# Reordering three groups of loads and casts in a windowed-attention and gated-FFN kernel

## The chip, the core and the metric

The kernel runs on one core of one Trainium2 chip. The metric is the device time of one execution in microseconds (us). It is taken over several runs, and one further execution is profiled.

The engines are named as in the profile: PE is TensorE (matmuls; PEld its weight loads), ACT is ScalarE, DVE is VectorE, POOL is GpSimd, and SP is SyncE, which here only issues DMAs. A "q" behind an engine's name means its instruction queue, which issues DMAs and waits.

## The reference

Attention over a batch of 4, with 8 heads, 768 positions and a head size of 64. Each position sees the first 4 positions (sinks) and the last 128. Its output, laid out as 3072 tokens by 512, goes through a gated feed-forward network:

```python
scores = scale * np.matmul(q, k.transpose(0, 1, 3, 2))
keep = is_sink | in_window              # rel = i - j, 0 <= rel < 128
a = softmax(np.where(keep, scores, -1e9))
x = np.matmul(a, v)                     # -> (3072, 512)
gate = np.maximum(x @ w_gate, 0.0)      # 512 x 1536
return (gate * (x @ w_val)) @ w_out     # 1536 x 512
```

All inputs and the output are float32 in device memory. The products run in bfloat16.

## The kernel before, in words

**Units.** The heads are taken in pairs, so a batch has four units, and there are 16 units U[0] to U[15]. Unit i belongs to batch i // 4 and pair i % 4. Of each unit the kernel needs the queries and keys turned to head size by position (`KQ`), the exponentials of the scores (`ee`), the product with the values (`xn`), and that product turned back (`xT`).

**Batch 0.** Its queries and keys come in eight halves: half c is pair c % 4, with c // 4 telling which half of the positions. `load_half` (L110) issues one load of k and one of q. `cast_half` (L116) casts them on GpSimd to bfloat16. `T_half` (L262) turns them on TensorE. So half 5 is the second half of pair 1. The float32 buffers `kf` and `qf` have three places, and half 5 uses the second part of the third.

**Batches 1 to 3.** Whole units are loaded by `load_rows` (L159) and cast by `cast_rows` (L164, on GpSimd). Batch 1 is turned on TensorE. For batches 2 and 3, `to_dram` (L169) writes the cast rows back to memory and `turn` (L174) reads them transposed. After that GpSimd copies "odd tiles" and sinks inside the keys (`odd_tiles` L183, `sinks` L179, the copies of L185 and L181), and the scores read those copies. `x_to_dram` (L147) and `x_turn` (L154) turn the attention output of batches 2 and 3 in the same way.

**Values.** There are seven value tiles a batch. `load_v` (L124) loads tile j with one DMA for even j and three for odd j, and `cast_v` (L133) casts it into `vn`, on GpSimd unless another engine is given. `W` (L310) is the product of exponentials and values. In batch 0 it is done in two parts: part 0 needs value tiles 0 to 2, part 1 needs tiles 3 to 6. In the other batches it needs all seven.

**Weights.** `load_w(m0, m1)` (L188) asks GpSimd's DMA queue for columns m0 to m1 (in blocks of 128) of `w_gate` and `w_val`, cast to bfloat16 on the way.

**The order.** Everything is in a hand-written order (`manual_schedule`), and each engine takes its instructions in program order. First comes an opening (L412 to L462) that brings up batch 0. Then follow 96 slots (L467): slot s does one `chunk` (L350), which is block m of the first FFN layer for one half of a batch's tokens: four matmuls with `w_gate`, four with `w_val` (L362), a relu on ACT (L377) and a product on DVE (L379). After its chunk, a slot does the attention steps that `plan` gives it ("S" scores, "W" value product, "X" and "T" turns, "H" turn of a half) and some matmuls of the second FFN layer (`ffn2`, L404). Ahead of its chunk, a slot does what `prep` gives it (L495 to L515): loads, casts and copies for later slots, in the order of the slot's list. Slots 0 to 23 are the FFN of batch 0, slots 24 to 47 of batch 1, and so on. Slot s of batch b runs while the attention of batch b + 1 is made.

Around the change the plan reads: slot 1 "S04 H1", slot 2 "S02 H2 S14", slot 6 "W01 W11" for batch 0 (L477); slot 29 "S00 S01", slot 31 "S02 S10", slot 35 "W0 S20" for batch 2 (L488). The scores of batch 0's first parts and the first value products stand in the opening. The row casts of unit 12 are in slot 33 (L504), and the odd tiles of a unit are copied in the slot ahead of its first scores (L508).

**Waits between engines** come from the data: a reader waits for its writer, a writer of a buffer for the buffer's readers. The memset of a corner of a float32 buffer (L138, L449) is used on purpose as a gate: it stands at a chosen point of DVE's order, and the load that overwrites the corner waits for it. Loads on SP share eight completion semaphores in turn, so a load on SP also waits until the load eight places earlier has landed.

Of the kernel before, what the change touches and what calls it, by code (L numbers as in the profile page):

```python
# [21 lines left out]
def kernel(  # L22
# [12 lines left out]
    nc = tc.nc  # L35
# [16 lines left out]
    kf = [const.tile([128, S], F32, name=f"kf{i}") for i in range(NQ)]  # L52
# [55 lines left out]
    half = lambda bufs, c: bufs[c // 2 % len(bufs)][:, c % 2 * HALF:c % 2 * HALF + HALF]  # L108

    def load_half(c, queues=(nc.sync, nc.sync)):  # L110
        p, x = c % NP, c // NP
        for src, bufs, queue in ((k, kf, queues[0]), (q, qf, queues[1])):
            queue.dma_start(out=half(bufs, c).rearrange("p (h e) -> p h e", h=2),
                              in_=src[0, 2 * p:2 * p + 2, x * HALF:x * HALF + HALF].rearrange("h (p n) d -> p h (n d)", n=3))

    def cast_half(c, copies=(nc.gpsimd.tensor_copy, nc.gpsimd.tensor_copy)):  # L116
        for src, dst, copy in ((kf, kn, copies[0]), (qf, qn, copies[1])):
            copy(half(dst, c).rearrange("p (n h d) -> p h n d", n=3, h=2),
                                  half(src, c).rearrange("p (h n d) -> p h n d", n=3, h=2))
# [4 lines left out]
    def load_v(b, j, r0=0, r1=128):  # L124
        r1 = min(r1, S - VROW[j])

        parts = [(0, 4, 0), (4, 16, VROW[j] + 4), (16, 128, VROW[j] + 16)] if j in (1, 3, 5) else [(0, 128, VROW[j])]
        for a0, a1, s0 in parts:
            a1 = min(a1, r1)
            if r0 <= a0 < a1:  # L130
                nc.sync.dma_start(out=vf[a0:a1, j, :, :], in_=v[b, :, s0:s0 + a1 - a0, :].rearrange("h s d -> s h d"))  # L131

    def cast_v(b, j, rows=128, copy=nc.gpsimd.tensor_copy):  # L133
        copy(vn[b % 2][0:rows, j, :, 0:64], vf[0:rows, j, :, :])  # L134
# [53 lines left out]
    def load_w(m0, m1, which=(0, 1)):  # L188
        for w, dst in (((moe_w_gate, wg), (moe_w_val, wv))[x] for x in which):
            nc.gpsimd.dma_start(out=dst[:, :, m0 * 128:m1 * 128],  # L190
                                in_=w.rearrange("(ko ki) n -> ki ko n", ki=128)[:, :, m0 * 128:m1 * 128])
# [5 lines left out]
    def setup():  # L197
        nc.vector.memset(warm[:], 0.0)
        nc.scalar.activation(warm[:], warm[:], Act.Exp, bias=0.0, scale=1.0)
        make_identity(nc, ident)  # L200

        nc.gpsimd.memset(band[:], 1.0)
        nc.gpsimd.affine_select(out=band[:], in_=band[:], compare_op=Alu.is_ge, fill=0.0, base=0,
                                pattern=[[1, 256]], channel_multiplier=-1)
        nc.gpsimd.affine_select(out=band[:], in_=band[:], compare_op=Alu.is_ge, fill=0.0, base=127,
                                pattern=[[-1, 256]], channel_multiplier=1)
        for c0, c1, x0 in ((8, 252, 0), (504, 507, 244)):
            nc.gpsimd.affine_select(out=msk[:, 0, c0:c1], in_=band[:, x0:x0 + c1 - c0], compare_op=Alu.is_ge, fill=0.0,
                                    base=119, pattern=[[0, c1 - c0]], channel_multiplier=-1)
        nc.gpsimd.memset(vf[:, 6, :, :], 0.0)  # L210
        cp, ms = nc.vector.tensor_copy, nc.vector.memset
        for i in range(NE):
            ms(ee[i][:, 0, :, 507:640], 0.0)
            ms(ee[i][:, 0, :, 0:8], 1.0)
        ms(vn[0][:, :, :, 64:66], 1.0)
        cp(msk[:, 0, 252:504], band[:, 4:256])
        ms(msk[0:4, 0, 252:504], 1.0)
        ms(msk[0:4, 0, 8:128], 1.0)
        ms(msk[0:4, 0, 128:252], 0.0)
        ms(msk[0:4, 0, 504:507], 0.0)  # L220
        bias(mb[:, 0, 8:507], msk[:, 0, 8:507])
        bias(mb[:, 1, 0:128], band[:, 0:128])
# [56 lines left out]
    def Sg(u, s, ps=None):  # L279
        t, bias = u.i % NT, u.b == 0 and s in (0, 3)  # L280
        g, b0, n, segs = SEG[s]
        ps = ps or pair()
        at = [ps[h][:] if isinstance(ps, list) else ps[:, h, :] for h in range(2)]
        if bias:
            for h in range(2):
                nc.tensor.matmul(out=at[h][:, b0:n], lhsT=ident[:], rhs=mb[:, g, b0:n], start=True, stop=False,
                                 skip_group_check=True)
        for x0, q0, c0, c1 in segs:
            for h in range(2):
                nc.tensor.matmul(out=at[h][:, c0:c1], lhsT=kE[t][64 * h:64 * h + 64, x0:x0 + 128],  # L290
                                 rhs=qT[t][64 * h:64 * h + 64, q0:q0 + c1 - c0], start=not bias, stop=True,
                                 skip_group_check=True)
        x = ee[u.i % NE][:, g, :, b0:n]
        if isinstance(ps, list):
            for h in range(2):
                nc.scalar.activation(x[:, h, :], at[h][:, b0:n], Act.Exp, bias=0.0, scale=scale)
        else:
            nc.scalar.activation(x, ps[:, :, b0:n], Act.Exp, bias=0.0, scale=scale)  # L298
        if not bias:
            nc.vector.tensor_tensor(x, x, msk[:, g, b0:n].unsqueeze(1).to_broadcast([128, 2, n - b0]), op=Alu.mult)  # L300
# [110 lines left out]
    with tc.manual_schedule():  # L411
# [3 lines left out]
            load_half(c, (nc.sync, nc.scalar))  # L415
        for j in range(3):
            load_v(0, j)
        for c in (4, 5):
            load_half(c)
        setup()  # L420
        g = [x[:] for x in G]
        dve = nc.vector.tensor_copy
# [13 lines left out]
        load_w(0, 2)  # L436
        for j in range(3):
            cast_v(0, j, copy=dve if j == 2 else nc.gpsimd.tensor_copy)
        load_w(2, 4)
        cast_half(4)  # L440
        cast_half(5)
        load_w(4, 6)
        Sg(U[2], 0, PP[1])
        Sg(U[2], 3, PP[0])
        W(U[0], 0, g[2])
# [47 lines left out]
                for y in w.split():  # L493
                    put(s, y, b)
        prep = [[] for _ in slots]  # L495
        prep[1] += [("half", 6), ("w", 6, 8), ("half", 7), ("setup3",), ("v", 0, 3), ("v", 0, 4), ("v", 0, 5), ("v", 0, 6)]
        prep[4] += [("load", 4), ("load", 5), ("load", 6)]
        prep[8] += [("kq", 4), ("load", 7), ("lv", 1), ("kq", 5), ("w", 8, 12)]
        prep[10] += [("kq", 6)]
# [9 lines left out]
            prep[at["W", i, 0] + 1].append(("xd", i))  # L509
            prep[at["W", i, 0] + 3].append(("xturn", i))  # L510

        for b, s0, s1 in ((2, 23, 28), (3, 44, 47)):
            for j in range(7):
                prep[s0 + j].append(("lv", b, j))
                prep[s1 + j].append(("v", b, j))  # L515

        f2 = deque()
        mid = {0: lambda: X(U[3], 0, g0), 8: lambda: X(U[3], 1)}
# [96 lines left out]
```

## Time and profile before

| | |
|---|---|
| median of 5 runs | 253.09 us (251.38 to 254.8) |
| the profiled execution, its own time | 254.61 us |
| its span in the profile | 252.6 us |
| granted TensorE clock, mean | 0.992 |
| TensorE busy | 239.1 us, 95% |
| DVE, ACT, GpSimd busy | 115.6, 120.6, 68.6 us |
| DMA | 40.07 MB, mean 159 GB/s |
| DMA queues: SP's, GpSimd's | 34.10 MB, 4.72 MB |
| chain that ended last: PE, DMA | 80%, 12% |

The span is the time from the first to the last instruction of the program; the execution's own time has about 2 us around it. Times "at" a moment are us from the start of the span. In lists of waits, the figures are total us, number of times, and the longest. In timelines, a bracket at the end of a line gives the idle time of the engine just before, and what ended it. The releaser is inferred from semaphore events. The DMA share of a stretch is the mean busy share of the core's 16 DMA engines; it can pass 1 since transfers overlap.

### The profile page before, as it was taken

The page shows a single profiled execution, that of the slowest core. Times are in us where ns is not written, and L with a number is a line of the kernel's source. Part 1 is how long each engine was busy: PE and PEld are TensorE (multiplying, and loading weights), DVE is VectorE, ACT ScalarE, POOL GpSimd, SP SyncE. Part 2 cuts the span into 40 slices and gives each one's busy share as a digit, 9 for nine tenths or more (in the row PEclk, how much of TensorE's full clock was granted, in tenths as well). Part 3 has the DMA queues.
Part 4 walks back from the last instruction along what each step waited for, and adds up shares of the span by engine and source line. Part 5 has one row for each costly group of instructions (what it writes and reads, how often), then busy time and mean ns, then how long its engine had stood idle before and what let it go on. Part 6 is the DMA issues. An engine that isn't in the chain of part 4 may idle for free.

```text
span 252.6 us, 5300 instructions
## 1 busy us (share of the span) xinstructions
PE 239.1 (95%) x2063; PEld 140.5 (56%) x2084; DVE 115.6 (46%) x224; ACT 120.6 (48%) x220; POOL 68.6 (27%) x125
## 2 busy tenths in 40 slices
PE   7879979999999997999999999999999999999994
PEld 3455566656765554566555556665555555555443
DVE  5465863788752443466434555734232223222000
ACT  3849927997343564453335754531333323333111
POOL 7775663982534305521003610000000000000000
PEclk9999999999999999799999999999999999999999
DMA  6999999999999999598899602334211011110232
GB/s 201 246 212 248 244 344 245 209 186 234 328 255 231 250 213 382 177 190 200 205 179 244 132 18 57 101 76 114 74 44 42 0 42 45 43 42 0 86 125 83
DMA packets 75681, 40.07 MB, mean 159 GB/s; under 512 B 53512, under 2 KB 72712, under 8 KB 75656
## 3 DMA queue, kind: packets, MB, share of 16 engines
q1 hardware_dynamic: 67560, 34.10, 52.3%
q0 software_dynamic: 6864, 4.72, 12.6%
q10 hardware_dynamic: 1232, 0.92, 1.1%
q8 instruction: 16, 0.26, 0.4%
q14 instruction: 9, 0.07, 0.1%
HBM read 28.48 MB, written 11.25 MB: 157 GB/s over the span
## 4 chain that ended last, share of the span: by engine, by line
PE 80%; DMA 12%; SPq 2%; issue 2%; POOL 1%; DVE 1%; ACT 1%; ACTq 0%; POOLq 0%; DVEq 0%
PE g L362 44%; PE g L404 19%; PE pp L325 5%; DMA vf<-in_v_dram 5%; DMA qf<-in_q_dram 4%; PE pp L290 4%; PE pp L404 3%; DMA kf<-in_k_dram 2%; SPq L131 1%; POOL vn L134 1%; PE g L342 1%; SPq L161 1%; PE pp L254 1%; PE g L254 1%; PE pp L398 1%
## 5 line engine op out<-in xcount | busy, mean ns | idle before, releaser
L379 DVE TENSOR_TENSOR hT<-gs,g 128x384 bf16<-128x384 f32 (+2 forms) x96 | 53.0, 552 | 89.7 <-PE g L362 81.2
L377 ACT ACTIVATE gs<-g 128x384 f32<-128x384 f32 (+2 forms) x96 | 47.7, 497 | 77.6 <-PE g L362 76.5
L362 PE MATMUL g<-xT,wv 128*128 128x384 bf16 (+2 forms) x384 | 79.1, 327 | 2.2 <-DMA wv<-in_moe_w_val_dram 2.2
L362 PE MATMUL g<-xT,wg 128*128 128x384 bf16 (+2 forms) x384 | 79.5, 328 | 0.5 <-ACT xT L345 0.5
L404 PE MATMUL g<-wo,hT 128*128 128x512 bf16 x219 | 61.0, 382 | 1.7 <-issue 0.5
L362 PEld LDWEIGHTS <-wg 128*128 128x128 bf16 x384 | 36.3, 98 | 31.1 <-issue 0.9
L362 PEld LDWEIGHTS <-wv 128*128 128x128 bf16 x384 | 37.5, 98 | 28.9 <-DMA wv<-in_moe_w_val_dram 3.1
L298 ACT ACTIVATE ee<-pp 128x838 bf16<-128x838 f32 (+4 forms) x50 | 43.0, 904 | 10.4 <-PE pp L290 9.9
L404 PEld LDWEIGHTS <-hT 128*128 128x128 bf16 x276 | 25.6, 98 | 24.1 <-issue 1.1
L300 DVE TENSOR_TENSOR ee<-ee,msk 128x838 bf16<-128x838 bf16 (+3 forms) x44 | 31.2, 711 | 14.2 <-ACT ee L298 13.4
L134 POOL CAST vn<-vf 128x512 bf16<-128x512 f32 x27 | 18.0, 682 | 32.7 <-DMA vf<-in_v_dram 32.7
L325 PEld LDWEIGHTS <-ee 128*128 128x128 bf16 x512 | 18.1, 97 | 5.5 <-issue 3.7
L325 PE MATMUL pp<-vn,ee 128*128 128x65 bf16 x488 | 18.1, 193 | 2.4 <-POOL vn L134 2.4
L408 ACT COPY ot<-g 128x512 f32<-128x512 f32 x20 | 11.7, 587 | 17.5 <-PE g L404 17.5
L331 DVE TENSOR_TENSOR xn<-pp,rn 128x896 bf16<-128x896 f32 (+2 forms) x18 | 17.0, 943 | 0.6
L290 PEld LDWEIGHTS <-KQ 64*128 64x128 bf16 x328 | 10.9, 94 | 10.2 <-issue 7.9
L290 PE MATMUL pp<-KQ 64*128 64x3 bf16 (+5 forms) x316 | 16.0, 222 | 0.0
L166 POOL CAST kn<-kf 128x768 bf16<-128x768 f32 x12 | 9.9, 828 | 19.2 <-DMA kf<-in_k_dram 10.8
L166 POOL CAST qn<-qf 128x768 bf16<-128x768 f32 x12 | 10.4, 865 | 3.5 <-DMA qf<-in_q_dram 3.4
L185 POOL COPY KQ<-KQ 128x372 bf16<-128x372 bf16 x12 | 6.8, 567 | 14.1 <-PE g L362 6.4
L345 ACT COPY xT<-g 128x372 bf16<-128x372 bf16 (+2 forms) x10 | 5.4, 545 | 7.2 <-PE g L342 7.2
L404 PE MATMUL pp<-wo,hT 128*128 128x512 bf16 x36 | 8.1, 379 | 0.0
(80 smaller groups left out, 107.0 us busy)
## 6 DMA issues: line engine op xcount, KB each, us to landing
out_dram<-ot SPq DMA_DIRECT2D x23, 256.0 KB
kf<-in_k_dram SPq DMA_DIRECT2D x12, 384.0 KB
qf<-in_q_dram SPq DMA_DIRECT2D x12, 384.0 KB
vf<-in_v_dram SPq DMA_DIRECT2D x12, 256.0 KB
vf<-in_v_dram SPq DMA_DIRECT2D x12, 224.0 KB
kf<-in_k_dram SPq DMA_DIRECT2D x8, 192.0 KB
wo<-in_moe_w_out_dram POOLq DMA_DIRECT2D x3, 512.0 KB, 9.1
kqd<-qn SPq DMA_DIRECT2D x8, 192.0 KB
```

The costliest lines, as they stand in the source:

```text
L134: copy(vn[b % 2][0:rows, j, :, 0:64], vf[0:rows, j, :, :])
L166: nc.gpsimd.tensor_copy(dst[u.i % 2][:].rearrange("p (n h d) -> p h n d", n=NR, h=2), src[u.i % NQ][:].rearrange("p (h n d) -> p h n d", n ...
L290: nc.tensor.matmul(out=at[h][:, c0:c1], lhsT=kE[t][64 * h:64 * h + 64, x0:x0 + 128], rhs=qT[t][64 * h:64 * h + 64, q0:q0 + c1 - c0], start ...
L298: nc.scalar.activation(x, ps[:, :, b0:n], Act.Exp, bias=0.0, scale=scale)
L300: nc.vector.tensor_tensor(x, x, msk[:, g, b0:n].unsqueeze(1).to_broadcast([128, 2, n - b0]), op=Alu.mult)
L325: nc.tensor.matmul(out=at[h][:, c:c + 65], lhsT=ee[u.i % NE][:, g, h, c0:c0 + 128], rhs=vn[u.b % 2][:, j, 2 * u.p + h, 0:65], start=c == 0 ...
L331: nc.vector.tensor_tensor(x.rearrange("p t (h d) -> p h t d", h=2), o[:, :, :, 0:64], r.unsqueeze(3).to_broadcast([128, 2, n, 64]), op=Alu ...
L362: nc.tensor.matmul(out=ps[:, 0:n], lhsT=w[:, ko, m * 128:(m + 1) * 128], rhs=x[:, ko, c], start=ko == 0, stop=ko == KO - 1)
L377: nc.scalar.activation(gs[:, 0:n], gp[:, 0:n], Act.Relu, bias=0.0, scale=1.0)
L379: nc.vector.tensor_tensor(h[:, m, c], gs[:, 0:n], vp[:, 0:n], op=Alu.mult)
L404: nc.tensor.matmul(out=op, lhsT=hT[b % 2][:, m, t * 128:(t + 1) * 128], rhs=wo[:, m, :], start=m == 0, stop=m == FM - 1)
L408: nc.scalar.copy(ot[:], op)
```

## The change

There are three edits.

1. The load of half 5 is taken out of the opening's first loads. It now stands behind the casts of value tiles 0 to 2, with a memset of its corner on DVE ahead of it, so that SP issues it once DVE has passed its own cast of value tile 2.
2. The loads of weights 4 and 5 are asked for ahead of the cast of half 5, and those of weights 6 and 7 ahead of the cast of half 6.
3. The casts of batch 2's value tiles 0 to 6 move from slots 28 to 34 into slots 27 to 33, and each stands first in its slot's list instead of last. Their loads stay where they were. The casts of batch 3 stay as they were.

```diff
         for j in range(3):
             load_v(0, j)
-        for c in (4, 5):
-            load_half(c)
+        load_half(4)
         setup()
...
         for j in range(3):
             cast_v(0, j, copy=dve if j == 2 else nc.gpsimd.tensor_copy)
+
+        nc.vector.memset(half(kf, 5)[0:1, 0:2], 0.0)
+        load_half(5)
         load_w(2, 4)
         cast_half(4)
+        load_w(4, 6)
         cast_half(5)
-        load_w(4, 6)
         Sg(U[2], 0, PP[1])
...
-        prep[1] += [("half", 6), ("w", 6, 8), ("half", 7), ("setup3",), ("v", 0, 3), ("v", 0, 4), ("v", 0, 5), ("v", 0, 6)]
+        prep[1] += [("w", 6, 8), ("half", 6), ("half", 7), ("setup3",), ("v", 0, 3), ("v", 0, 4), ("v", 0, 5), ("v", 0, 6)]
...
-        for b, s0, s1 in ((2, 23, 28), (3, 44, 47)):
+        for b, s0, s1 in ((2, 23, 27), (3, 44, 47)):
             for j in range(7):
                 prep[s0 + j].append(("lv", b, j))
-                prep[s1 + j].append(("v", b, j))
+                prep[s1 + j].insert(0 if b == 2 else len(prep[s1 + j]), ("v", b, j))
```

## The prediction

> **What bounds the kernel now.** I read the page first (TensorE busy 239.1 of 252.6 us), then the chain of waits by line, then who waits for whom on TensorE, then the timeline at the places that the diff touches. The waits on TensorE:
>
> ```profile
> PE pp L325 <- POOL vn L134: 2.4, 4, 1.0
> PE g L362 <- DMA wv<-in_moe_w_val_dram: 2.2, 2, 1.1
> ```
>
> So TensorE sets the end, and it loses time at few places: at the value casts (total us, times, longest us) and at two weight loads. The opening, from the timeline of TensorE (start, us, work, idle before it and its releaser):
>
> ```profile
> 18.22 0.49 PE L362 MATMUL g<-xT,wv 128*128 128x372 bf16 x2 [1.05 <-DMA wv<-in_moe_w_val_dram]
> 32.41 0.80 PE L362 MATMUL g<-xT,wv 128*128 128x372 bf16 x4 [1.12 <-DMA wv<-in_moe_w_val_dram]
> 33.61 0.22 PE L325 MATMUL pp<-vn,ee 128*128 128x65 bf16 x2 [0.21 <-POOL vn L134]
> 34.17 1.12 PE L325 MATMUL pp<-vn,ee 128*128 128x65 bf16 x32 [0.34 <-POOL vn L134]
> ```
>
> Two weight waits, then a release by the value casts at 34.17. The second place is slot 35, the first value product of batch 2. The timeline of GpSimd there:
>
> ```profile
> 88.32 0.61 POOL L134 CAST vn<-vf 128x512 bf16<-128x512 f32 x1 [0.90 <-DMA vf<-in_v_dram]
> 97.39 0.83 POOL L166 CAST kn<-kf 128x768 bf16<-128x768 f32 x1 [8.45 <-DMA kf<-in_k_dram]
> 98.42 0.83 POOL L166 CAST qn<-qf 128x768 bf16<-128x768 f32 x1 [0.21 <-DMA qf<-in_q_dram]
> 99.19 0.61 POOL L134 CAST vn<-vf 128x512 bf16<-128x512 f32 x1
> 99.75 0.50 POOL L185 COPY KQ<-KQ 128x372 bf16<-128x372 bf16 x1
> 100.19 0.19 POOL L181 COPY KQ<-KQ 128x12 bf16<-128x12 bf16 x1
> 100.33 0.61 POOL L134 CAST vn<-vf 128x512 bf16<-128x512 f32 x1
> ```
>
> GpSimd stands 8.45 us at the key cast of unit 12, and the last two value casts (tiles 5 and 6) stand behind it. They were asked for at 87.71 to 89.47, and the completion events in the trace put their landing at 92.2 and 92.3. What TensorE does meanwhile, from the same timeline:
>
> ```profile
> 99.86 0.22 PE L325 MATMUL pp<-vn,ee 128*128 128x65 bf16 x2 [0.97 <-POOL vn L134]
> 100.99 0.70 PE L325 MATMUL pp<-vn,ee 128*128 128x65 bf16 x18 [0.91 <-POOL vn L134]
> ```
>
> And its clock by the microsecond (the granted clock is the first figure after the busy times):
>
> ```profile
> 101.00:102.00 1.00, 1.00 (x24) 0.80 (x23) 0.25 (x1) 0.00 (x0) 1.00 (x2) 0.88 0.88 328
> 102.00:103.00 1.00, 0.78 (x6) 0.39 (x4) 0.99 (x1) 0.82 (x1) 1.00 (x3) 0.50 0.20 71
> 103.00:104.00 1.00, 1.00 (x4) 0.37 (x4) 0.79 (x2) 0.18 (x1) 0.06 (x1) 0.50 0.07 25
> 104.00:105.00 1.00, 1.00 (x5) 0.48 (x4) 0.00 (x0) 0.16 (x1) 0.34 (x1) 0.50 0.61 146
> 105.00:106.00 1.00, 1.00 (x14) 0.51 (x14) 0.20 (x1) 0.33 (x1) 1.00 (x2) 0.91 0.62 133
> ```
>
> Nearly 2 us of standing are followed by half a clock from about 101.8 to 105.2. The missing clock adds up to 0.12 + 0.5 + 0.5 + 0.5 + 0.09 = 1.71 us.
>
> **What the Trainium skill says.** "TensorE: Matmul & The Clock Gate", What's actually happening: the clock falls to half after a mostly idle window of 3413 ns and returns after a busy one; the windows run freely. The trace agrees in the half (0.50) and the length (3.4 us), and shows that about 2 us of idleness can do it. Same page, Architectural detail: GpSimd takes its queue strictly in order; the 8.45 us agree. "DMA: Bandwidth & Descriptors", Issuing engines are not separate DMA queues: loads from SP and GpSimd share the same 16 engines; and Queues, rings and completion order: an engine takes turns among its queues. The trace agrees: from 12 us to 34 us the DMA share is at or above 1.0.
>
> **The change, part by part.**
>
> *Batch 2's values a slot sooner, ahead of their slot's other work.* Same seven casts of 0.61 us. Tile 6 now stands in slot 33 ahead of unit 12's row casts, tile 5 in slot 32. Both run at 92.2 to 93.4 in what was GpSimd's idle 8.45 us. Slot 35's product then runs at 98.35 in 0.97 us, as the other 32-matmul products do, instead of until 101.69: 3.34 - 0.97 = 2.37 us saved. Late next: scores S20 of the same slot read unit 10's odd tiles, which GpSimd copies after unit 12's casts. Those end at about 99.2 as before, since their load sets them; the copies follow without the value cast between, 99.19 + 0.44 + 0.19 = 99.82. The product ends at 99.32 and S20's first pair takes about 0.15, so its second pair waits 0.35 to 0.4 us. Net 1.97 us. With one short wait the clock should hold. From the product's end to the next chunk's end took 105.70 - 101.69 = 4.0 us; at full clock scores 0.5, three FFN2 matmuls 0.7 and chunk 1.30 make 2.5. That is 1.5 us more; in runs of before whose clock held, this part is nothing.
>
> What the sooner casts push back: unit 8's odd-tile copy now stands behind value tiles 0 and 1 (tile 1 landed at 81.0), so it ends at 82.4 instead of 78.6; its scores start at 84.79. Unit 9's stands behind tiles 2 and 3 (tile 3 landed at 86.5), so it ends at 87.9; its scores start at 89.35. Both cost nothing, with 2.4 and 1.4 us of cover; each us beyond costs a us. SP's order is untouched here. Afterwards SP is nearly continuously issuing from 110.7 to 133, and the last turned x of batch 2 landed at 132.2, 0.2 us before its chunk at 132.40. SP's stretch starts when slot 37's product is normalised, so it moves up with TensorE; I count no loss, at most 1 us.
>
> *Half 5 asked for behind the first values.* One DVE memset (0.06 us, the row of L449) behind the third value cast, which ends at 12.29 + 0.48 = 12.77. The k load goes out at about 12.9 instead of 10.12, q at 13.4 instead of 10.63. Behind it on SP stands only half 6, which waits for its own memset until 15.2 anyway. Memset cost: nothing, DVE idles until 13.34. The first weights get the engines alone meanwhile. k and q of half 5 are 0.39 MB at some 0.32 MB/us, 1.2 us. So wv for slots 0 and 1 lands about 1.1 us sooner and the 1.05 us wait at 18.22 goes. Half 5 was cast by 17.7 and is transposed at 21.8; 2 to 2.5 us later it still fits.
>
> *Weights ahead of casts.* Each pair of loads holds GpSimd 1.5 us (0.74 + 0.75). Weights 4 and 5 go out near 14.9 instead of 17.64, 6 and 7 near 19.5 instead of 22.96. The casts behind each pair start 1.5 us later and land within the waits for their loads.
>
> *What of that reaches the end.* Product W01 at 34.17 waits for value tiles 3 to 6 of batch 0, which land at about 33 because the same bytes (weights 0 to 7, eight halves, all values) have to pass full engines first. A reordering doesn't shorten this sum. So TensorE arrives 1 to 2 us sooner and waits as much longer: 0 gained, between -1 (values land sooner because weights no longer trail on some engines) and +1.7 (the longer standing halves the clock for one window).
>
> **Sum.** 1.97 + 1.5 + 0 = 3.5 us. Against the profiled execution's own 254.61 (span 252.6 and 2.0 around it) that is 251.1. The median of the five runs, 253.09, is 1.5 lower; they spread over 3.4 us, which fits a clock drop that not every run has, so at the median 2.0 to 3.5 is gained. I take 3.2: 249.9.
>
> **Rivals.**
> *Both places gain.* Values land 1 us sooner and W01 follows. For: weights trail on some engines to 32.4. Against: full engines. 253.09 - 4.3 = 248.8.
> *The opening gives back.* The longer standing before W01 (some 2.5 us, where 1.12 + 0.55 stood) costs half a clock, 1.5 us: 249.9 + 1.5 = 251.4. For: 1.9 us did it at slot 35. Against: windows run freely and need not fall so.
> *The wait moves to S20.* The row load of unit 12, or its copies, come a us or more later relative to TensorE, the wait is as long as before and the clock falls too: under 1 us is left, 252.3. Against: its load is issued by SP, whose chain starts at a gate that TensorE's progress opens, near 60 us.
> *Slower: weights push the values.* With weights 6 and 7 queued 3.5 us sooner the weight queue never runs dry (it nearly did at 19 to 21), and the values of batch 0 give way by a full pair: 0.52 MB at 0.185 MB/us (the rate in 16 to 18, with weights alone) is 2.8 us, plus half a clock after it, 1.5: 249.9 + 4.3 = 254.2. It decides from a landing 3.2 us late, after 36.2. Against: those weights passed ahead of the last values before, too.
> That the change does nothing: excluded for the casts, whose order is GpSimd's program order.
>
> **How the numbers follow.** Forecast 0.55 (its own range 248.8 to 251.0), both gain 0.13, opening gives back 0.17, wait moves 0.09, slower 0.06. Leaving out a tenth on each side gives 248.4 to 252.8. One per cent, about what a measurement of this kernel can tell from no change, is 2.5 us, so faster begins at 250.6: three quarters of the forecast, all of "both", a fifth of "gives back": 0.57. Slower (above 255.6) 0.04, the far ends of the last two rivals; the rest 0.39.
>
> **What would show it.** Right: value casts of tiles 5 and 6 ahead of the 8 us gap on GpSimd; no wait for vn in slot 35; at most 0.5 us before S20; clock 1.00 through 106; wait at 18.22 gone; W01 still released by a value cast near 34. Wrong: a new TensorE wait for unit 8's or 9's odd tiles, a half clock near 34 to 38, or value tile 5 of batch 0 cast much after 33.

## The result, and the profile after

The changed kernel takes 253.29 us (median of 44 runs, 251.14 to 257.13) where the kernel before, run beside it, takes 252.88 (79 runs, 250.93 to 256.38). The ratio is 1.0019, 95% interval 1.0002 to 1.0036: no gain, where 3.2 us were forecast. Here and below, ratios leave out the runs that took over 1.5% longer than the fastest run of their kernel, while the medians are over all runs. The profiled execution of the changed kernel took 252.6 us by its own time, with a span of 250.5 and a granted clock of 1.000.

That is 2 us below the profiled execution of before (254.61), and still no gain: the profile of before was one of the longer executions of its kernel. The table sets them side by side with a second profile of before (before_again) and others that are used below. A slot's start is its first matmul of L362. Each column is one execution.

| start of (us) | before | before_again | after | after_timed | third edit alone (values_again) |
|---|---|---|---|---|---|
| slot 7 | 35.12 | 34.39 | 34.44 | 35.75 | 34.91 |
| slot 19 | 60.77 | 60.03 | 60.07 | 61.39 | 60.55 |
| slot 20 | 63.19 | 63.14 | 63.64 | 66.08 | 62.98 |
| slot 35 | 97.05 | 97.00 | 97.49 | 99.94 | 96.84 |
| slot 36 | 103.31 | 101.73 | 101.04 | 103.29 | 100.19 |
| slot 52 | 141.56 | 139.15 | 139.46 | 140.61 | 137.51 |
| end of the span | 252.57 | 250.18 | 250.46 | 251.61 | 248.51 |

The waits on TensorE of the changed kernel (total us, times, longest):

```profile
PE pp L325 <- POOL vn L134: 1.9, 4, 0.7
...
PE pp L290 <- POOL KQ L181: 0.6, 1, 0.6
...
PE g L362 <- DMA xT<-xd: 0.3, 1, 0.3
```

The weight loads (wv) have left the list. The value casts are still there, with 1.9 us where 2.4 stood, so either the third edit failed or they wait elsewhere. The timeline of GpSimd ahead of slot 35 shows that the edit did what it says:

```profile
93.56 1.18 POOL L134 CAST vn<-vf 128x512 bf16<-128x512 f32 x2 [2.97 <-DMA vf<-in_v_dram]
97.55 0.83 POOL L166 CAST kn<-kf 128x768 bf16<-128x768 f32 x1 [2.81 <-DMA kf<-in_k_dram]
98.70 0.83 POOL L166 CAST qn<-qf 128x768 bf16<-128x768 f32 x1 [0.33 <-DMA qf<-in_q_dram]
99.47 0.50 POOL L185 COPY KQ<-KQ 128x372 bf16<-128x372 bf16 x1
99.91 0.20 POOL L181 COPY KQ<-KQ 128x12 bf16<-128x12 bf16 x1
```

Tiles 5 and 6 are cast by 94.74, ahead of the row casts of unit 12. TensorE there, and its clock by the microsecond:

```profile
98.79 1.13 PE L325 MATMUL pp<-vn,ee 128*128 128x65 bf16 x32
99.86 0.59 PE L290 MATMUL pp<-KQ 64*128 64x244 bf16 x6
```

```profile
101.00:102.00 1.00, 1.00 (x7) 0.59 (x6) 0.79 (x2) 0.62 (x2) 0.82 (x2) 1.00 1.05 395
102.00:103.00 1.00, 1.00 (x19) 0.58 (x17) 0.61 (x2) 0.50 (x2) 1.00 (x2) 1.00 1.10 408
```

The product runs in one piece, S20 waits for 0.2 us at most, the clock stays at 1.00. In the opening the wait at 18.22 is gone (the first line, the same two matmuls, has no bracket) and W01 is released by a value cast again, at 33.47 where it was 34.17:

```profile
16.71 0.48 PE L362 MATMUL g<-xT,wv 128*128 128x372 bf16 x2
...
32.55 0.22 PE L325 MATMUL pp<-vn,ee 128*128 128x65 bf16 x2 [0.39 <-POOL vn L134]
33.47 1.12 PE L325 MATMUL pp<-vn,ee 128*128 128x65 bf16 x32 [0.70 <-POOL vn L134]
```

All this is as forecast. What was not is slot 19, where batch 1's first value product stands. Its line in the kernel before, and its lines in the changed one:

```profile
62.23 1.13 PE L325 MATMUL pp<-vn,ee 128*128 128x65 bf16 x32
```

```profile
62.54 0.22 PE L325 MATMUL pp<-vn,ee 128*128 128x65 bf16 x2 [0.48 <-POOL vn L134]
63.10 0.70 PE L325 MATMUL pp<-vn,ee 128*128 128x65 bf16 x18 [0.34 <-POOL vn L134]
```

Before, nothing waits. After, TensorE waits twice for the last two value tiles of batch 1; from slot 19 to slot 20 it takes 3.57 us instead of 2.42. In the table the same stretch takes 4.69 us in after_timed. The casts of these tiles on GpSimd wait for their loads, in both kernels; the last one before, then the last two after:

```profile
61.97 0.61 POOL L134 CAST vn<-vf 128x512 bf16<-128x512 f32 x1 [0.36 <-DMA vf<-in_v_dram]
```

```profile
61.88 1.17 POOL L134 CAST vn<-vf 128x512 bf16<-128x512 f32 x2 [5.75 <-DMA vf<-in_v_dram]
```

The last cast ends at 62.58 before and at 63.05 after, 0.47 us later. The rest of the new wait is there because TensorE reaches slot 19 0.70 us sooner in this profile. So what counts is how late slot 20 begins.

The later loads begin in SP's timeline (start, us, work, count). Before, then after:

```profile
18.29 9.07 SPq L131 DMA_DIRECT2D vf<-in_v_dram  x8
27.45 0.39 SPq L161 DMA_DIRECT2D kf<-in_k_dram  x1
```

```profile
18.05 11.52 SPq L131 DMA_DIRECT2D vf<-in_v_dram  x8
29.67 0.39 SPq L161 DMA_DIRECT2D kf<-in_k_dram  x1
```

SP issues the last eight DMAs of batch 0's values from nearly the same moment, but it needs 11.52 us for them instead of 9.07, and so the first rows of batch 1 (L161) are asked for 2.2 us later. Nearly all of it is the issues' own time (10.81 and 8.46 us); it is not the wait for the load eight places earlier, since the longest issue, 4.17 us from 21.74, began after the last signal of that load at 21.63.

The delay of the issue does not go on to the end of the queue: the last row load and the first value load of batch 1 go out at 35.87 and 36.28 after, and at 36.04 and 36.46 before. The bytes are behind for longer: by 36 us the queue of SP had moved 5.87 MB before and 5.46 after, by 40 us 7.17 and 6.98, and by 44 us the same (7.64 and 7.63). The issue of the last value load of batch 1 ends at 51.17 before and at 51.75 after. At that time w_out begins to pass, asked for by GpSimd, and the values that are left come slowly: in the profile of before SP's queue moved only some 0.27 MB from 52 to 60 us, where it had moved 0.34 a us at 32 to 40. So a small lateness there has a price.

### The profile page after: what moved, and what is told of

The parts are those of the page before. It is cut to its first block, busy times and chain, and to the rows that moved or that the text cites. A ratio compares the mean times of both kernels' runs of the same rounds, so it can differ in the third digit from the quotient of the medians.

```text
span 250.5 us, 5303 instructions
## 1 busy us (share of the span) xinstructions
PE 237.4 (95%) x2063; PEld 140.1 (56%) x2084; DVE 115.8 (46%) x225; ACT 120.9 (48%) x220; POOL 69.9 (28%) x125
## 3 DMA queue, kind: packets, MB, share of 16 engines
q1 hardware_dynamic: 67560, 34.10, 52.7%
## 4 chain that ended last, share of the span: by engine, by line
PE 70%; DMA 20%; SPq 4%; issue 2%; POOL 1%; DVE 1%; ACTq 0%; ACT 0%; POOLq 0%; DVEq 0%
PE g L362 37%; PE g L404 19%; DMA vf<-in_v_dram 14%; PE pp L325 5%; DMA qf<-in_q_dram 4%; PE pp L404 3%; SPq L131 3%; PE pp L290 3%; DMA xd<-xn 1%; DMA xT<-xd 1%; SPq L113 1%; PE pp L398 1%; PE g L398 1%; POOL vn L134 1%; PE g L342 0%
## 5 line engine op out<-in xcount | busy, mean ns | idle before, releaser
L362 PE MATMUL g<-xT,wg 128*128 128x384 bf16 (+2 forms) x384 | 79.0, 326 | 0.8 <-ACT xT L345 0.5
L362 PE MATMUL g<-xT,wv 128*128 128x384 bf16 (+2 forms) x384 | 78.7, 326 | 0.0
L362 PEld LDWEIGHTS <-wg 128*128 128x128 bf16 x384 | 36.1, 98 | 30.3
L362 PEld LDWEIGHTS <-wv 128*128 128x128 bf16 x384 | 37.6, 98 | 26.2 <-issue 1.8
L134 POOL CAST vn<-vf 128x512 bf16<-128x512 f32 x27 | 18.7, 711 | 40.2 <-DMA vf<-in_v_dram 40.2
```

The costliest lines, as they stand in the source:

```text
L362: nc.tensor.matmul(out=ps[:, 0:n], lhsT=w[:, ko, m * 128:(m + 1) * 128], rhs=x[:, ko, c], start=ko == 0, stop=ko == KO - 1)
```

## The experiments

**Both kernels once more.** No edit; a second profile of each, because the profile of before held a half clock.

> The kernel before, profiled once more on another occasion. If its first profile is typical (theory A: the late value casts and the half clock in slot 35 are in most executions), it shows a wait of 1.5 to 2.5 us for vn in slot 35 and a half-clock window near 102 again, span near 252.6. If its first profile was an unlucky one (theory B), there is no half clock there, slot 48's chunk starts 1.5 to 3 us sooner than 132.2, and a wait for the turned x or for odd tiles shows in slots 48 to 51, which the first profile did not have.

> The changed kernel, profiled once more. Both theories: no wait for vn in slot 35, a wait before S20 of 0.1 to 1 us at most, and waits of 0.3 to 1.5 us in all in slots 48 to 51, where the first profile of it had a wait for the turned x (0.34) and for unit 13's odd tiles (0.64).

Measured: 252.2 us (span 250.2) and 252.46 (span 250.3). The second profile of before has slot 35's wait, but no half clock:

```profile
100.11 0.70 PE L325 MATMUL pp<-vn,ee 128*128 128x65 bf16 x18 [0.91 <-POOL vn L134]
```

That is between the two theories. Slots 35 to 36 take 4.73 us in it, 1.38 above the 3.35 of values_again; in the profile that the prediction was read from they took 6.26. After_again loses 2.1 us at slot 19.

**The edits apart.** The third edit alone, and the first two alone.

```diff
-        for b, s0, s1 in ((2, 23, 28), (3, 44, 47)):
+        for b, s0, s1 in ((2, 23, 27), (3, 44, 47)):
...
-                prep[s1 + j].append(("v", b, j))
+                prep[s1 + j].insert(0 if b == 2 else len(prep[s1 + j]), ("v", b, j))
```

> Edit 3 alone: batch 2's value casts a slot sooner and first in their slots. Theory A (the gain is there, and the opening gives it back): 0.8 to 1.4% faster, ratio 0.986 to 0.992. Theory B (a later wait, set by SP's queue and by the order on GpSimd in slots 48 to 51, takes what slot 35 gains): ratio 0.997 to 1.002, with no vn wait in slot 35 and new TensorE waits at slots 48 to 51.

Measured: 0.9937 of before (0.9905 to 0.9969), 251.45 against 253.47 us, between the two theories.

> Edits 1 and 2 alone: half 5 gated and the weights ahead of the casts. Theory A: 0.8 to 1.4% slower, ratio 1.008 to 1.014, through a half clock near 34 or value tiles 3 to 6 landing later than 33. Theory B: ratio 0.999 to 1.004; the wait at 18 for wv is gone, and the release of W01 stays within 1 us of 34.2.

Measured: 1.0025 (0.9996 to 1.0054), theory B's range, with W01 at 34.36. Its profile loses 0.83 us at slot 19, and at slot 35 only 0.7 are lost instead of 1.38: slot 35 begins later, and waits less. Slot 36 begins at 102.13, against 101.73 in before_again.

So the third edit gains 0.6% by itself, and with the other two beside it the gain is gone, though these two alone cost only 0.25%, with an interval that holds 1. They were then divided. Edit 1 alone (half 5 behind the first values):

```diff
-        for c in (4, 5):
-            load_half(c)
+        load_half(4)
...
+        nc.vector.memset(half(kf, 5)[0:1, 0:2], 0.0)
+        load_half(5)
```

> Edit 1 alone: half 5 asked for behind the first values, the order of weights and casts as before. If the weights' order carries the opening's cost (theory C1), ratio 0.996 to 1.001, with the wv wait near 17 gone and SP's queue at least 6.5 MB in by 36 us. If the late half carries it (theory C2, SP's queue stands empty from 12 to 16 us and never catches up), ratio 1.002 to 1.006 and about 6.2 MB by 36 us.

Edit 2 alone (weights ahead of casts):

```diff
         load_w(2, 4)
         cast_half(4)
+        load_w(4, 6)
         cast_half(5)
-        load_w(4, 6)
...
-        prep[1] += [("half", 6), ("w", 6, 8), ("half", 7), ...
+        prep[1] += [("w", 6, 8), ("half", 6), ("half", 7), ...
```

> Edit 2 alone: weights 4 to 7 ahead of the casts, half 5 asked for as before. Theory C1 (the value loads, packets of 256 B, ride alone behind the weights and pass slower than beside them): ratio 1.002 to 1.006, W01's release 34.2 or later. Theory C2: 0.996 to 1.001.

Measured: 1.0025 (0.9995 to 1.0054) and 1.0026 (1.0003 to 1.0049). The first ratio is what theory C2 said, the second what C1 said, so neither theory holds for both, and a cost of edit 1 isn't shown. The profiles differ. With edit 1 alone the weights stand behind casts that now come later, and TensorE pays in the opening (in an execution of 255.45 us, where the median is 253.48):

```profile
35.30 1.11 PE L362 MATMUL g<-xT,wv 128*128 128x372 bf16 x3 [2.86 <-DMA wv<-in_moe_w_val_dram]
```

SP issues its eight value DMAs in 6.22 us there. With edit 2 alone TensorE waits for no weights behind slot 0 (0.83 us there), but the eight take 11.96 us. So it is the sooner weights that hold SP up. This profile of edit 2 loses only 0.23 us at slot 19, so the hold-up alone does not fix what is lost there.

**Is slot 19 the place? The loads of w_out moved.** GpSimd asks for w_out in three loads ahead of batch 1's value casts; here they stand between casts 4 and 5, in the kernel with the third edit alone and in the changed one.

```diff
-        prep[13] += [("wo",)]
-        prep[14] += [("v", 1, 0), ("v", 1, 1), ("v", 1, 2), ("v", 1, 3), ("v", 1, 4), ("v", 1, 5), ("v", 1, 6)]
+        prep[14] += [("v", 1, 0), ("v", 1, 1), ("v", 1, 2), ("v", 1, 3), ("v", 1, 4), ("wo",), ("v", 1, 5), ("v", 1, 6)]
```

> Edit 3, and the three loads of w_out moved on GpSimd from slot 13 to between the value casts 4 and 5 of batch 1 (slot 14), where GpSimd arrives near 56.8 instead of 49. Theory C (slot 19's wait for batch 1's last values is a floor that the DMA engines set, since w_out passes beside tile 5): tile 5 lands at 57 to 59.5 instead of 61 to 63, no vn wait in slot 19, slot 20 starts by 63.2, ratio 0.988 to 0.993. Theory D (the floor is elsewhere): slot 20 unchanged and the ratio as for edit 3 alone, 0.992 to 0.996, or above if w_out is now late for the second FFN layer.

> The changed kernel with the same move of w_out. Theory C (the opening's cost acts only through slot 19's floor): within 0.3% of the run with edit 3 and the move, ratio 0.987 to 0.994. Theory D (the opening edits cost on their own, by a half clock or by later values of batch 0): 0.5% or more slower than that run.

Measured: 1.0167 (1.011 to 1.0224) and 1.019 (1.0148 to 1.0232). Both are slower than either theory said. The wait at slot 19 is gone in both, so w_out's bytes take part in it. But the lateness has only moved on; TensorE in slot 29 of the first kernel (the second has 3.75 us there):

```profile
87.55 0.85 PE L290 MATMUL pp<-KQ 64*128 64x252 bf16 x10 [3.38 <-POOL KQ L181]
```

Unit 8's odd tiles are late, since their copy on GpSimd stands behind value tiles 0 and 1 of batch 2, and tile 1 lands late: its cast begins at 86.30, the copy at 86.86. That is the wait for unit 8's odd tiles that the prediction named as a sign of being wrong. (The expectations further down speak of slot 31 and unit 9 for it.)

**Repeats, and two variants of the third edit.** The third edit alone and the changed kernel again without an edit; then only tiles 5 and 6 sooner; then the third edit with two places of small waits moved, unit 10's odd tiles ahead of unit 12's row casts and batch 3's value casts a slot later.

```diff
-                prep[s1 + j].append(("v", b, j))
+                if b == 2 and j > 4:
+                    prep[s1 - 1 + j].insert(0, ("v", b, j))
+                else:
+                    prep[s1 + j].append(("v", b, j))
```

```diff
-            prep[at["S", i, 0] - 1].append(("sinks", i))
+            if i == 10:
+                prep[33].insert(0, ("sinks", i))
+            else:
+                prep[at["S", i, 0] - 1].append(("sinks", i))
...
-        for b, s0, s1 in ((2, 23, 27), (3, 44, 47)):
+        for b, s0, s1 in ((2, 23, 27), (3, 44, 48)):
```

> Edit 3 alone, timed a second time beside the changed kernel. Theory E (edit 3 gains where the wait of slot 35 stands and the opening's two edits then take it back): ratio 0.990 to 0.997 again, at least 0.4% below the changed kernel of this job. Theory F (the two belong to different occasions and the first difference was chance): within 0.3% of the changed kernel.

> The changed kernel beside it. Theory E: ratio 0.998 to 1.004, and slot 7 and slot 20 of its profile later than those of edit 3 alone by some 0.5 us. Theory F: ratio as for edit 3 alone.

> Of edit 3 only value tiles 5 and 6 of batch 2, put first in slots 32 and 33; tiles 0 to 4 stay where they were. Theory G (the gain is only that these two stand ahead of unit 12's row casts): the same ratio as edit 3 alone within 0.3%, 0.990 to 0.997, no vn wait in slot 35. Rival (the sooner casts of tiles 0 to 4 matter, or cost): more than 0.4% off.

> Edit 3, with unit 10's odd-tile copy also put ahead of unit 12's row casts (front of slot 33), and the value casts of batch 3 a slot later (slots 48 to 54), behind unit 13's odd tiles. Theory H (what takes slot 35's place is S20's wait for that copy and slot 50's for unit 13's): no wait before S20 and none for odd tiles in slot 50, 0.2 to 0.4% below edit 3 alone, ratio 0.987 to 0.994. Rival (the loads, not the order on GpSimd, end last there): no difference to edit 3 alone beyond 0.2%.

Measured: 0.9969 (0.9939 to 0.9999), 1.002 (0.9995 to 1.0045), 0.9976 (0.9953 to 0.9998) and 0.9964 (0.9941 to 0.9988). So the gain came again, with an interval that ends just short of 1. Tiles 5 and 6 alone are within the interval of the whole edit, and in their profile slot 35 has no wait for a value cast. But it waits 1.06 us before S20 there (102.53), because unit 12's row cast came at 100.09, 2.5 us later than the 97.55 of the changed kernel; this execution had a half clock in the opening. The changed kernel's small waits at slots 48 to 51 (the 0.3 and 0.6 us in its list) are not what takes the gain back: without such places the third edit is no better. Slot 19 of after_timed:

```profile
64.99 0.22 PE L325 MATMUL pp<-vn,ee 128*128 128x65 bf16 x2 [1.60 <-POOL vn L134]
```

From slot 19 to 20 the four profiles with the whole opening and w_out in its place lose 0.83, 1.15, 2.10 and 2.27 us, 1.6 in the mean. The six with neither of its edits lose 0.3 in the mean (four of them nothing, before_again 0.69, values_only 1.17). Two of these four reach slot 19 some 2 us later than the rest, with a half clock behind them, which hides a wait. Without them it is four against four: slot 7 begins at 34.9 in the mean without the opening's edits and at 35.0 with them, slot 20 at 63.4 and at 64.7. That is 1.3 us, most of it at slot 19.

**Does the opening cost anywhere else?** First with the least move, one w_out load behind the last value cast of batch 1, on the third edit alone and on the changed kernel:

```diff
-        prep[13] += [("wo",)]
-        prep[14] += [("v", 1, 0), ... ("v", 1, 6)]
+        prep[13] += [("wo", 0, 1)]
+        prep[14] += [("v", 1, 0), ... ("v", 1, 6), ("wo", 2)]
```

> The third edit alone (batch 2's values sooner), and only the third load of w_out is moved, from slot 13 to behind value cast 6 of batch 1 in slot 14. Theory (what the opening's edits cost, they cost through slot 19, where TensorE waits for batch 1's last values): here that wait is at most 0.1 us, and the time is 0.990 to 0.997 of the kernel before, with no new wait at slot 31. Rival (a debt of the transfers that only changes its place): TensorE waits 1 us or more at slot 31 for unit 9's odd tiles, as it did when all three loads were moved, and the time is 1.000 to 1.010.

> The changed kernel with all three edits, and the same move of the third load of w_out. Theory (slot 19 is the only way by which the opening's edits reach the end): the wait at slot 19 falls from 1.2 to 2.3 us to at most 0.5, and this kernel comes within 0.3% of the run beside it that has the third edit alone with the same move. Rival (they cost elsewhere, in the clock or later): slot 19 has no wait, and this kernel is still 0.5% or more slower than the run beside it. Second rival: the debt only changes its place, and slot 31 waits 1 us or more in both.

Measured: 1.0064 (1.0025 to 1.0102) and 1.0058 (1.0031 to 1.0086). The two agree, but this doesn't decide: TensorE waits for odd tiles at later slots in both (1.8 us at slots 35 and 50 in the first, 3.0 at slots 29, 31 and 35 in the second). The debt has moved on, though not to slot 31 in both as the second rival said, and a wait that takes in a delay can hide a difference. So bytes were taken out instead. First one of the three loads:

```diff
-                                         rhs=wo[:, i, c], start=i == 0, stop=i == FM - 1)
+                                         rhs=wo[:, i % 8, c], start=i == 0, stop=i == FM - 1)
...
-        nc.tensor.matmul(out=op, lhsT=hT[b % 2][:, m, t * 128:(t + 1) * 128], rhs=wo[:, m, :],
+        nc.tensor.matmul(out=op, lhsT=hT[b % 2][:, m, t * 128:(t + 1) * 128], rhs=wo[:, m % 8, :],
...
-                    for c in range(3):
+                    for c in range(2):
```

> The third edit alone, and the third of w_out's three loads is left out: blocks 8 to 11 of the second FFN layer use blocks 0 to 3 of w_out instead, so its output isn't the reference's; the instructions of TensorE, DVE and ACT stay as many. About 1 MB less passes beside batch 1's last values and the loads after them, so neither slot 19 nor slot 31 should have a wait. Expected: 0.990 to 0.996 of the kernel before, at the level of the third edit alone (0.9937 and 0.9969) or a little below.

> The changed kernel with all three edits, and the third of w_out's loads left out in the same way (blocks 8 to 11 use blocks 0 to 3; the output isn't the reference's). Theory (the opening's edits cost only by the transfers that they leave behind, and that shows first at slot 19): slot 19 waits at most 0.4 us, slot 31 not at all, and this kernel comes within 0.3% of the run beside it with the third edit alone and the same load left out. Rival (they cost in the opening itself, by its waits or the clock there): no wait at slots 19 and 31, and this kernel is still 0.5% or more slower than the run beside it.

Measured: 0.9935 (0.9912 to 0.9959) and 0.9986 (0.996 to 1.0012). Neither profile waits at slot 19, 29 or 31, and they are 0.5% apart: by what was written down, the rival's side. The two profiles say so too: the second ends 1.03 us later, and 0.93 of that is there at slot 7 (35.14 against 34.21). But batch 1's last cast ended at 62.09 in the second, and the product began at 62.24; an execution with an opening sooner by more than 0.15 us would have waited there. So all three loads were taken out:

```diff
-                                         rhs=wo[:, i, c], start=i == 0, stop=i == FM - 1)
+                                         rhs=wv[:, i % 4, c], start=i == 0, stop=i == FM - 1)
...
-        nc.tensor.matmul(out=op, lhsT=hT[b % 2][:, m, t * 128:(t + 1) * 128], rhs=wo[:, m, :],
+        nc.tensor.matmul(out=op, lhsT=hT[b % 2][:, m, t * 128:(t + 1) * 128], rhs=wv[:, m % 4, 0:d_model],
...
-        prep[13] += [("wo",)]
```

> The third edit alone, and none of w_out is loaded: the second FFN layer multiplies by columns of w_val instead, so its output isn't the reference's; the instructions of TensorE, DVE and ACT stay as many, GpSimd issues three DMAs fewer. Some 3 MB less passes ahead of and beside batch 1's last values, whose casts should end before 60. Expected: 0.990 to 0.996 of the kernel before, no wait at slots 19, 31 and 35.

> The changed kernel with all three edits, and w_out left out in the same way (the second FFN layer multiplies by columns of w_val; the output isn't the reference's). With one load left out, batch 1's last cast still ended at 62.09, 0.15 us ahead of slot 19's product, so that place could still bind in executions whose opening is sooner. Theory (slot 19 is all that the opening's edits cost): batch 1's last cast ends 1 us or more ahead of slot 19's product, and this kernel comes within 0.3% of the run beside it. Rival (part of the cost is in the opening itself): it stays 0.35% or more slower, and slot 7 starts later by as much.

Measured: 0.9919 (0.9885 to 0.9953) and 0.9914 (0.989 to 0.9938). They agree. SP's timeline shows that the hold-up in the opening is still there, the third edit alone first:

```profile
17.36 9.51 SPq L131 DMA_DIRECT2D vf<-in_v_dram  x8
26.97 0.39 SPq L161 DMA_DIRECT2D kf<-in_k_dram  x1
```

```profile
18.29 12.57 SPq L131 DMA_DIRECT2D vf<-in_v_dram  x8
30.96 0.39 SPq L161 DMA_DIRECT2D kf<-in_k_dram  x1
```

The rows of batch 1 are asked for 4 us later, and slot 19 doesn't wait, because the values of batch 1 are ready: all seven casts of the second kernel end at 60.56 and slot 19's product begins at 64.40 (this execution had a half clock from 35.7, which costs TensorE some 1.7 us). The times are on the theory's side. But the sign that was written down for the rival is there in the one profile of each: slot 7 begins at 35.65 against 34.78, 0.87 us or 0.35% later. And the two intervals together leave room for some 0.4% either way, about the size of what was looked for. Leaving w_out out also relieves every later load, not slot 19 alone.

So the two experiments don't say the same. Taking only the runs whose mean granted clock is 0.997 or more, the first pair is 0.9 us apart (251.31 against 250.44 in the mean of 12 and 14 runs), the second is not (251.06 against 251.22, 15 and 7 runs). w_out is asked for after slot 7, so moving it or leaving it out does not touch the opening, and more profiles can be set side by side there: slot 7 begins at 34.4 to 35.8, 35.2 in the mean of eight, with both edits, and at 34.2 to 35.1, 34.7 in the mean of seven, with neither (only profiles whose clock held till then). About 0.5 us in the opening and 1 us at slot 19 would fit all of it; that split is an estimate from these figures and not shown.

## Why the prediction was wrong

**The third edit: mechanism right, size wrong.** The step read "2.37 us saved", less "0.35 to 0.4" before S20, and 1.5 more for the clock. The casts moved, the wait went, S20 waited less than forecast, and the two pieces of cover on unit 8's and 9's odd tiles held: no new wait at slots 29 and 31. But it gained 0.3 and 0.6% (0.9969 and 0.9937), about 0.8 to 1.6 us of some 253, not 3.5. The steps that failed are the two terms of the sum, 1.97 and 1.5, both too large:
- The wait. In before_again slot 35 loses 1.38 us where the first profile has 2.91 (6.26 - 3.35, half clock and all). Less the 0.2 that the changed kernel loses there, 1.2 us are left. The times agree: among runs with a mean clock of 0.997 or more, the third edit gains 1.2 us in both timings (251.24 against 252.47, and 251.09 against 252.33, in the mean).
- The clock. The prediction noted that in runs whose clock held this part is nothing, and then took most of it. Of the 252 runs of before beside these experiments, 119 (47%) have a mean granted clock below 0.997, a sign of a half-clock window (one of 3.4 us brings the mean to 0.993); of 48 runs with the whole third edit on the opening of before, 20 (42%). So the edit does not take most of these windows away. In the profiles that have one, they began at 101.8 (before), but at 19.0, 34.6, 34.8, 34.8, 35.7, 86.4 and 89.2 in others: four of eight at the waits around W01. Taking a gap out at slot 35 leaves those gaps. The prediction's "mostly idle window" is also wider than the page it cites: the Trainium skill, "TensorE: Matmul & The Clock Gate", What's actually happening, has the half clock after an idle window. In the trace of before, 1.88 us of standing (0.97 and 0.91) came ahead of it, and before_again stood 0.91 us at the same place and kept its clock.

**Edits 1 and 2: right at W01, wrong beyond it.** The step that failed is "0 gained", with the sentence "a reordering doesn't shorten this sum" as its reason. Up to W01 it is nearly right: the wait at 18.22 went, TensorE waits longer at W01, and slot 7 begins 0.5 us later in the mean (35.2 against 34.7), within the prediction's own "between -1 and +1.7". The claim that the later casts "land within the waits for their loads" is not: TensorE waits 0.90 and 0.34 us for casts of queries at 23.75 and 26.66, which the wait at W01 then takes in.

But the sum ended at W01. SP issues the loads of batch 1 behind those of batch 0, and its issue is held up: 8.1 to 9.6 us for the eight value DMAs in nine of the ten profiles with the opening of before (11.4 in the tenth, whose clock fell at 19 us), 10.4 to 13.2 in all nine that ask for the weights sooner. The issue of batch 1's values then ends at 51.8 to 54.0 us in the five profiles with the sooner weights and w_out in its place, and at 51.1 to 52.7 in four with the opening of before (those with a clock that held till slot 19); their last cast ends at 63.1 to 65.5 and at 61.6 to 63.7. At slot 19 the cover was nearly nothing: the last cast ended at 62.58 in the profile of before, and the product that began at 62.23 ran on without a wait. That is one look at a timeline that the prediction didn't take; it followed a moved load to its first reader, not to the next loads of its queue. All the signs that the prediction named for being right were seen, clock and waits alike; they all lay at the two places where it had looked.

**The rivals.** The slower one, "weights push the values", has the mechanism half right: the weights do push SP's values, by 2 to 3 us of issue. It put the price at batch 0's product, with a point of decision at 36.2; W01 came at 33.47, and the price fell due a batch later. "The wait moves to S20" and "the opening gives back" by a half clock are not what happened to the changed kernel. The first shows 0.2 us there; it did come, with 1.1 and 1.3 us, in two profiles of the variants (tiles56_only and values_wo1), both with a half clock in the opening. For the second, the share of runs with a lower clock is 26 of 66 (39%), no more than before; that its 1.5 us is close to what the opening cost is luck. The price of the SP stretch from 110.7 to 133, "no loss, at most 1 us", is borne out: 0.3 us for a turned x at slot 48 in one profile of the changed kernel, and 0.2 and 0.5 us in two of the variants.

**Why the gain and the cost meet.** In the kernel before, slot 35 waits anyway, and a delay at slot 19 can shorten that wait. The profile of opening_only shows it: it is 1.1 us behind before_again at slots 20 and 35, and 0.4 behind at slot 36. That is one profile, and not every delay is taken in: half5_only is 3.3 us behind at slot 35, from its waits in the opening, and still loses 1.31 us there. Once the third edit has taken slot 35's wait away, every microsecond at slot 19 reaches slot 36 (slot 20 to 36 takes 37.2 to 37.4 us in all profiles with the whole edit and w_out loaded in its place; 38.6 in before_again). Gain 1.2, loss 1.3 by slot 20: about nothing, and 0.4 us slower was measured. Neither term is known to better than some 0.5 us, by the spread of the runs and profiles.

**The best version** that computes the reference is the third edit alone, 0.9937 and 0.9969, ahead of the kernel before by less than 1% and of the changed kernel beside it (1.002). Its two variants, 0.9976 and 0.9964, can't be told from it.

**Open.** How the cost of the first two edits divides between the opening and slot 19 isn't settled. Why the sooner weights hold SP's issue up was not measured by itself either. "DMA: Bandwidth & Descriptors" of the Trainium skill, Queues, rings and completion order, says that a DMA engine takes turns among its queues; the traces fit that (more weights in the queue beside the values, fewer values through), but no run shows a queue being full. Nor was a version tried that has the opening's edits and asks for batch 1's values ahead of its rows.

## What to carry to other kernels

A load that is asked for sooner can push back what stands behind the loads that it competes with, not only the next reader: follow the queue to the next batch, and write down the slack at each later place that reads from it. Gains at two waits in a row need not add up: the later one can hide a delay at the earlier, and taking it out uncovers what it hid. And a half clock in one profile is not a price until a second profile of the same kernel has it in the same place.

## What was unexpected

- One DMA issue on SP can take as long as a wait, without waiting for a semaphore: of the eight value DMAs in the changed kernel the shortest took 0.32 us and the longest 4.17. SP's line for that group (min/median/max ns):

```profile
L131 SPq DMA_DIRECT2D vf<-in_v_dram x8: 322/470/4171, 18.1 to 27.0; - x8
```

- About half the runs of one and the same kernel have a lower mean clock (below 0.997) and half don't, and their medians are 1.4 to 2.5 us apart (252.0 to 252.7 against 253.4 to 254.6 for before, by group of runs).
